# A first layer of 20 block products a pair instead of 22, chained over PSUM banks

## The chip, the cores and the metric

The kernel runs on one core of a Trainium2 chip (trn2). TensorE is called PE here, VectorE DVE, ScalarE ACT, GpSimd POOL and SyncE SP. The metric is the time of one execution in microseconds (us), as the median of several runs on the device.

## The reference

Two stages in float32. The first is a linear attention with the delta rule, for 4 batches of 8 heads, 768 steps and 48 features a head. Its output is laid out as 3072 tokens of 384 features. The second is a feed-forward network with a gate, of width 2048:

```python
for t in range(S):
    kt, vt, bt = (k_n[:, :, t], v[:, :, t], beta[:, :, t, None])
    y[:, :, t] = np.einsum('bhd,bhde->bhe', q[:, :, t], state)
    v_old = np.einsum('bhde,bhd->bhe', state, kt)
    state = state + bt[:, :, :, None] * np.einsum('bhd,bhe->bhde', kt, vt - v_old)
...
h = x @ w_in            # 3072 x 384 by 384 x 2048
g = h * np.cos(h)
return (g @ w_out)      # 3072 x 2048 by 2048 x 384
```

## The kernel before

**Tiling.** The 768 steps are cut into 24 units of 32 steps; a unit of all 4 batches is 128 tokens. Two units make a pair: 12 pairs of 256 tokens.

**The attention, by units.** `turn` and `gram` on PE make the products of keys and queries. The grams go through DRAM (`gram_put`, `gram_get`) into a tile `gb`, and POOL inverts a triangular matrix for two units at once: `invert`, whose lines L765 and L772 run one after the other for each of 32 columns in narrowing shapes, in a tile `z` that ACT first sets to the identity (L744). The result goes through DRAM again (`put`, L786, then `get`, L805) into `zt`, and PE runs `solve`, `update` and `within`, and `features`, which turns the result into `x_ffn`, the input of the network: three blocks of 128 features for each of the pair's two units. Inversion m serves the units 2m and 2m+1. SP issues most transfers; 16 stand on ACT's queue.

**The network, by pairs.** The first layer's weights `w_in` are three rows (k = 0 to 2) of sixteen 128x128 tiles. They come in parts: the load is split, shifted and added together, the last of it on POOL (L547), which does the same for `w_out`. Pairs 0 and 1 run the first layer plainly (`hidden`, L965: for each of 8 groups of four tiles, twelve matmuls into one PSUM bank). Pairs 2 to 11 use a bilinear scheme: tiles are taken four at a time, as one block of 128 by 512, so that a product is four 128x128 matmuls into one bank. In the trace one float32 matmul shows as two records. A plain pair would take 24 such products. The scheme takes 11 for each half `s` of the width, 22 in all. For it, sums of blocks of x are made for each pair (`x_sum`, L1046, four DVE operations on 128x128) and sums of weight blocks once (`in_sums`, L1061, eight DVE operations on 128x512). `layer` (L1084) runs the products of step i, `layer_out` copies a bank into the gate tile on ACT (L1100) or adds the gate tile and a bank on DVE (L1103), so that partial sums are used more than once.

**Gating and the second layer.** Each 128x512 block of h then goes through `turns` on ACT (L1005), `rest` on DVE (L1012), `cos` on ACT (L1021) and `gate` on DVE (L1024). The second layer of pair 0 is plain (`output`, L1110); the other pairs use seven products instead of eight (`product`, L1167, each in two halves of four matmuls of 128x192; sums of gate blocks on DVE, L1183; `collect`, L1217).

**PSUM.** Eight banks: two for `kq`, two for `two`, three for `h` (the first layer's), one for `o`.

**Order.** Every piece of work is a task with an engine, a cost and what it depends on. `Order.run` plays them through at build time as a list scheduler with due times, small corrections for each kind of task, and a set of tasks on ACT's queue. The order in which it starts them is the order in which they are emitted, and each engine keeps its own. So PE's order mixes first-layer products of a pair, second-layer halves of the pair before, and attention steps of later units.

Of the kernel before, what the change touches and what calls it, by code (L numbers as in the profile page):

```python
# [11 lines left out]
FP = mybir.dt.float32  # L12
# [5 lines left out]
C = 32  # L18
# [29 lines left out]
class Order:  # L48

    WINDOW = 1261.351
    LAG = {"PE": 0.2, "DVE": 0.15, "ACT": 0.15, "POOL": 0.2, "SP": 2.0, "IN": 0.0}


    RING, ISSUE, LANES = 128, 0.49, 8
    DESCRIPTORS = {
        "weights": 8, "gram_put": 64, "gram_get": 4, "put": 128, "blocks": 32, "store": 8,
        "store_left": 8, "store_right": 8,
    }

    STEADY, LATE = 130.0, {'SP': 0.66, 'POOL': 1.21, 'ACT': 0.3, 'DVE': 0.15}
    SLOW, WARM = 1.7, 4.0
    STICK = 2.528  # L70
    CHANGE = 0.17

    EARLY, NUDGE = 6, {('hidden', True): 61.2, ('out', False): 7.4, ('layer', False): 5.9, ('within', False): -4.5, ('hidden', 0, 8): 32.3, ('right', True): -39.1, ('inv', 0, 3): 5.0, ('solve_out', True): -66.4, ('turn', False): 28.3, ('rest', False): 22.3, ('rest', True): -14.8, ('state', False): -8.9, ('layer', True): 9.7, ('solve', True): 4.8, ('left', True): -6.1, ('left', False): 11.8, ('weigh', False): 11.0, ('cos', True): -11.4, ('inv', True): 4.0, ('update', False): -3.7, ('gate', False): 5.6}


    ON_ACT = {('weights', 9): 1, ('gram_put', 0): 1, ('weights', 14): 1, ('weights', 3): 1, ('gram_get', 1): 1, ('k', 7): 1, ('k', 4): 1, ('q', 3): 1, ('weights', 10): 1, ('gram_get', 2): 1, ('weights', 15): 1, ('weights', 5): 1, ('weights', 17): 1, ('weights', 6): 1, ('put', 0): 1, ('gram_get', 0): 1}
    HOLD = {('v', 5): 82.16, ('k', 8): 77.57, ('add', 9): 86.94, ('norms', 1, 1): 28.35, ('rest', 0, 2): 87.09, ('k', 6): 50.8, ('gate', 0, 4): 90.29, ('split', 11): 68.31, ('shift', 4): 40.04, ('eye', 1): 46.45, ('weights', 14): 75.83, ('features', 1): 93.82, ('split', 8): 56.33, ('split', 10): 65.61, ('get', 2): 96.99, ('half_out', 0): 53.13, ('split', 13): 77.98, ('shift', 5): 40.52, ('gram', 0): 16.72, ('norms', 2, 0): 49.12, ('add', 10): 91.37, ('add', 8): 66.01, ('right', 2): 94.14, ('q', 5): 52.19, ('add', 3): 36.15, ('square', 1, 0): 17.78, ('gram_queries', 2): 46.41, ('shift', 1): 23.89, ('shift', 16): 96.85, ('hidden', 0, 0): 70.69, ('gram_queries', 1): 23.15, ('split', 17): 99.7, ('add', 12): 77.47, ('get', 3): 101.36, ('weigh', 1): 61.19, ('v', 2): 42.92, ('eye', 2): 99.51, ('weights', 2): 18.93, ('gram_put', 2): 29.69, ('hidden', 0, 4): 80.59, ('turn_out', 1): 13.43, ('shift', 9): 60.15, ('weights', 1): 13.99, ('gram_keys', 3): 39.3, ('scale', 0, 0): 13.88, ('square', 3, 0): 65.52, ('turn', 0): 9.1, ('weigh', 0): 44.66, ('scale', 0, 1): 14.96}
    PAIRED = (
        "square", "sum", "norms", "scale", "weigh", "gram_get", "eye", "inv", "inv_out", "put",
        "x_sum", "layer", "layer_out", "turns", "rest", "cos", "gate", "out", "left", "collect",  # L80
        "store", "out_out",
    )
    SMALL = ("solve_half", "between", "gram", "state", "solve", "update", "within")


    BLOCK, PHASE, AHEAD, FETCH = 256, 63, 38, 3.5
    COUNT = {
        "turn": 16, "gram": 128, "state": 256, "solve": 128, "solve_half": 128, "between": 128, "update": 64, "within": 128,
        "features": 6, "hidden": 48, "out": 16,
    }  # L90

    def __init__(self, bufs, free):
        self.bufs, self.free = bufs, free
        self.tasks, self.users, self.tiles = {}, {}, {}
        self.written, self.rest, self.there = 0, 0.0, {}

    def add(
        self, key, engine, cost, emit, deps=(), makes=(), uses=(), moves=0.0, due=1e9
    ):

        assert key not in self.tasks, key
        if key in self.ON_ACT:
            assert moves
            engine = "ACT"
        self.tasks[key] = [engine, cost, due, emit, set(deps), makes, uses, moves]
        for t in uses:
            self.users[t] = self.users.get(t, 0) + 1
        for tag, t in makes:
            self.tiles[t] = tag

    def count(self, key):
        if key == ("state", 0):
            return 0
        if key[0] == "layer":
            return 32 if key[3] in (1, 6, 7) else 16
        return self.COUNT[key[0]]

    def descriptors(self, key):
        n = self.DESCRIPTORS.get(key[0], 16)
        if key[0] in ("k", "gram_put") and key[1] >= 8:  # L120
            n //= 2
        return n

    def stall(self, key, now, commit):

        n = count = self.count(key)

        n = int(n * 1.034 if self.written < 1000 else n * 1.0054 + self.rest)
        cost, stall, there = self.tasks[key][1], 0.0, {}
        for i in range(self.written + 1, self.written + n + 1):  # L130
            t = now + cost * (i - self.written) / n + stall
            if (i + self.PHASE + self.AHEAD) % self.BLOCK == 0:
                there[(i + self.PHASE + self.AHEAD) // self.BLOCK + 1] = (
                    t + self.FETCH + (1.5 if t < self.STEADY else 0.0)
                )
            if (i + self.PHASE) % self.BLOCK == 0:
                block = (i + self.PHASE) // self.BLOCK
                stall += max(0.0, there.get(block, self.there.get(block, 0.0)) - t)
        if commit:
            if self.written >= 1000:  # L140
                self.rest += count * 1.0054 - n
            self.written += n
            self.there.update(there)
        return stall

    def run(self, wrote):
        waiting, heirs, ready = {}, {}, {e: [] for e in self.LAG}
        for key, task in self.tasks.items():
            waiting[key] = len(task[4])
            for d in task[4]:  # L150
                heirs.setdefault(d, []).append(key)

        left = {key: len(heirs.get(key, ())) for key in self.tasks}
        ends = [key for key, n in left.items() if n == 0]
        for key in ends:
            engine, cost, due, *_, moves = self.tasks[key]
            for d in self.tasks[key][4]:
                t = self.tasks[d]
                t[2] = min(t[2], due - t[1] - self.LAG[t[0]] - t[7])
                left[d] -= 1  # L160
                if left[d] == 0:
                    ends.append(d)
        for key, task in self.tasks.items():
            n = key[1] if len(key) > 1 and isinstance(key[1], int) else 0
            if key[0] in self.PAIRED:
                n *= 2
            task[2] += self.NUDGE.get((key[0], n < self.EARLY), 0.0) + self.NUDGE.get(key, 0.0)
        for count, (key, task) in enumerate(self.tasks.items()):
            if not task[4]:
                heapq.heappush(ready[task[0]], (task[2], count, key))  # L170
        live = {tag: 0 for tag in self.bufs}
        left = dict(self.users)
        free = {e: self.free.get(e, 0.0) for e in self.LAG}
        flights, accepted, hot = [(7.0, 7.5, 8, "SP")] * self.LANES, {}, 1e9
        running, small = {}, False
        events = [(t, 0, None, False) for t in sorted({0.0, *free.values(), *self.HOLD.values()})]
        heapq.heapify(events)
        count, now = len(self.tasks), 0.0
        log = []
        while events:  # L180
            now, _, key, done = heapq.heappop(events)
            if key is not None:
                if done:
                    del running[key]
                    for t in self.tasks[key][6]:
                        left[t] -= 1
                        if left[t] == 0:
                            live[self.tiles[t]] -= 1
                engine, moves = self.tasks[key][0], self.tasks[key][7]
                for h in heirs.get(key, ()):  # L190

                    near = self.tasks[h][0] == engine and not moves
# [1458 lines left out]
```

## Time and profile before

Three runs: 670.58, 672.70 and 676.12 us.

| What | before |
|---|---|
| median of the runs | 672.70 us |
| profiled execution, first to last instruction (span) | 668.2 us; the page has no other time of this execution |
| TensorE clock granted, mean | 0.998 |
| PE busy, MATMUL records | 615.3 us (92%), 12120 |
| DVE busy, instructions | 470.1 us (70%), 892 |
| ACT busy, instructions | 246.2 us (37%), 416 |
| POOL busy, instructions | 348.5 us (52%), 734 |
| DMA moved | 51.8 MB, mean 78 GB/s |

How to read it. A group's line gives the source line, engine, operation, output and inputs, shape, count, then the busy time and the mean of one in ns, then the idle time of that engine just before, with what ended it. Records of PE overlap, so the mean of one is longer than the time from one to the next. The chain is the work that ended last, followed back from the end. In the slices a digit is tenths of busy time, 40 slices of 16.7 us each. A line of the waits gives what waited and for what, then total us, times, and the longest. In the timeline, the first number is the start, the second the duration.

### The profile page before, as it was taken

Reading aid. Unit: us, or ns where it says so; the run is one execution under the profiler, and the core shown is the slowest. Engines: PE = TensorE matmul, PEld = TensorE weight load, DVE = VectorE, ACT = ScalarE, POOL = GpSimd, SP = SyncE. Lnnn points to the kernel's source line nnn. Section 1 sums busy time; section 2 is a strip of 40 time slices with the busy share of each in tenths; the row PEclk is TensorE's granted clock in tenths of the full one; section 3 lists DMA queues with packets and bytes.
Section 4 is the critical chain, followed back from the end, with each engine's and each line's share of the span. In section 5 each row is a group of like instructions: output and inputs, shape, how many; then the busy total and the mean of one; then the engine's idle time right before and its main releaser. Section 6 shows DMA issues by size and latency. Waiting matters only on the chain.

```text
span 668.2 us, 27726 instructions
## 1 busy us (share of the span) xinstructions
PE 615.3 (92%) x12120; PEld 576.3 (86%) x12120; DVE 470.1 (70%) x892; ACT 246.2 (37%) x416; POOL 348.5 (52%) x734
## 2 busy tenths in 40 slices
PE   3316999999999999999999999999999999999997
PEld 3315878887989998999999999989999999989996
DVE  6695679788775875977866867767667656656661
ACT  3433545651243342433434334333324324323420
POOL 4458788978728628458438477158077067000000
PEclk9999999999999999999999999999999999999999
DMA  8866764574455244344434343342311311100000
GB/s 174 205 162 147 180 150 118 135 126 68 73 97 83 51 80 76 53 87 75 64 70 72 67 79 60 63 79 46 71 29 44 50 27 34 25 3 26 1 25 24
DMA packets 215645, 51.80 MB, mean 78 GB/s; under 512 B 207076, under 2 KB 210420, under 8 KB 215524
## 3 DMA queue, kind: packets, MB, share of 16 engines
q1 hardware_dynamic: 204516, 43.39, 34.4%
q10 hardware_dynamic: 10752, 6.20, 3.5%
q8 instruction: 95, 1.56, 1.0%
q0 software_dynamic: 256, 0.44, 0.3%
q14 instruction: 26, 0.21, 0.1%
HBM read 39.24 MB, written 10.75 MB: 75 GB/s over the span
## 4 chain that ended last, share of the span: by engine, by line
PE 82%; POOL 5%; DMA 5%; DVE 4%; issue 2%; ACT 1%; SPq 1%; ACTq 0%; DVEq 0%; POOLq 0%
PE p_h L1084 31%; PE p_out L1167 29%; PE p_kq L822 4%; PE p_h L965 3%; PE p_out L1110 3%; PE p_s L908 2%; PE p_u L885 2%; PE p_kq L925 2%; PE p_g L655 2%; POOL part L765 2%; POOL z L772 2%; PE p_o L1167 2%; PE p_z L944 1%; DMA g_dr<-g 1%; DMA qp<-in_q_dram 1%
## 5 line engine op out<-in xcount | busy, mean ns | idle before, releaser
L765 POOL TENSOR_TENSOR part<-z,gb 128x126 f32<-128x126 f32 (+22 forms) x341 | 135.8, 398 | 134.5 <-DMA gb<-g_dr 77.9
L772 POOL TENSOR_TENSOR z<-z,part 128x126 f32<-128x126 f32 (+22 forms) x341 | 138.5, 406 | 26.7
L1084 PE MATMUL p_h<-x_ffn,w_in 128*128 128x128 f32 x1120 | 145.5, 277 | 1.0 <-issue 1.0
L1084 PEld LDWEIGHTS p_h<-x_ffn,w_in 128*128 128x128 f32 x1120 | 135.5, 192 | 3.7 <-issue 2.1
L1167 PE MATMUL p_out<-w_out,g_ffn 128*128 128x192 f32 x672 | 122.9, 327 | 0.3 <-issue 0.3
L1005 ACT ACTIVATE turns<-p_h,quarter_turn 128x512 int32<-128x512 f32 x96 | 66.0, 687 | 150.3 <-DVE p_h L1103 106.9
L1167 PEld LDWEIGHTS p_out<-w_out,g_ffn 128*128 128x128 f32 x672 | 107.6, 190 | 1.0 <-issue 0.6
L1167 PE MATMUL p_out<-w_sum,g_ffn 128*128 128x192 f32 x496 | 91.3, 329 | 0.0
L1021 ACT ACTIVATE turns<-turns,halfpi 128x512 f32<-128x512 f32 x96 | 69.1, 721 | 42.3 <-DVE turns L1012 40.9
L1012 DVE SCALAR_TENSOR_TENSOR turns<-p_h,turns 128x512 f32<-128x512 f32 x96 | 65.6, 683 | 26.9 <-ACT turns L1005 26.8
L1167 PEld LDWEIGHTS p_out<-w_sum,g_ffn 128*128 128x128 f32 x496 | 79.4, 190 | 1.0
L1183 DVE TENSOR_TENSOR g_ffn<-g_ffn 128x512 f32<-128x512 f32 x88 | 61.9, 704 | 14.8 <-PE p_out L1167 13.9
L1100 ACT COPY g_ffn<-p_h 128x512 f32<-128x512 f32 x60 | 35.2, 586 | 96.4 <-PE p_h L1084 96.1
L1103 DVE TENSOR_TENSOR p_h<-g_ffn,p_h 128x512 f32<-128x512 f32 x60 | 41.7, 695 | 38.6 <-PE p_h L1084 37.8
L1024 DVE TENSOR_TENSOR g_ffn<-turns,p_h 128x512 f32<-128x512 f32 x96 | 64.9, 678 | 5.5 <-POOL w_out L547 3.3
L576 POOL TENSOR_TENSOR knrm<-ksum,halves 128x16 f32<-128x16 f32 (+1 forms) x14 | 37.3, 2665 | 39.8 <-DVE ksum L564 39.8
L965 PE MATMUL p_h<-x_ffn,w_in 128*128 128x128 f32 x384 | 47.7, 283 | 1.5 <-POOL w_in L547 1.3
L965 PEld LDWEIGHTS p_h<-x_ffn,w_in 128*128 128x128 f32 x384 | 45.3, 196 | 2.7 <-POOL w_in L547 1.7
L1217 DVE SCALAR_TENSOR_TENSOR o<-p_out,o 128x192 f32<-128x192 f32 x74 | 25.3, 354 | 29.5 <-PE p_out L1167 29.0
L1084 PE MATMUL p_h<-x_sum,in_sum 128*128 128x128 f32 x320 | 43.1, 278 | 0.7 <-issue 0.7
L1084 PEld LDWEIGHTS p_h<-x_sum,in_sum 128*128 128x128 f32 x320 | 40.2, 191 | 1.4 <-issue 0.8
L624 PE MATMUL p_t<-consts,kp 128*128 128x128 f32 x32 | 7.4, 373 | 31.8 <-DMA halves_z<-z_dr 19.4
(110 smaller groups left out, 780.4 us busy)
## 6 DMA issues: line engine op xcount, KB each, us to landing
pairs<-in_moe_w_out_dram SPq DMA_DIRECT2D x13, 384.0 KB
vp<-in_v_dram SPq DMA_DIRECT2D x96, 48.0 KB
gb<-g_dr SPq DMA_DIRECT2D x18, 256.0 KB
out_dram<-o SPq DMA_DIRECT2D x23, 192.0 KB
pairs<-in_moe_w_in_dram SPq DMA_DIRECT2D x7, 512.0 KB
kp<-in_k_dram SPq DMA_DIRECT2D x128, 24.0 KB
z_dr<-z SPq DMA_DIRECT2D x11, 256.0 KB
zt<-z_dr SPq DMA_DIRECT2D x88, 32.0 KB
```

The costliest lines, as they stand in the source:

```text
L576: nc.gpsimd.tensor_tensor(out=scales[m][2][:, part], in0=sums[m, part.start][:, 0:n], in1=halves[:, 0:n], op=ALU.pow,)
L765: eng.tensor_tensor(out=part, in0=z[:, 0:rows, j, None].to_broadcast(shape), in1=a[:, j, None, j + 1 :].to_broadcast(shape), op=ALU.mult,)
L772: eng.tensor_tensor(out=behind, in0=behind, in1=part, op=ALU.subtract)
L965: nc.tensor.matmul(p_h[:, i], w_in[:, t, (4 * k + i) * 128 : (4 * k + i + 1) * 128], xts[p][:, t, unit * 128 : (unit + 1) * 128], start=(t ...
L1005: nc.scalar.activation(turns[p, f], hidden_of(p, f), AF.Identity, bias=quarter_turn, scale=TURN)
L1012: nc.vector.scalar_tensor_tensor(out=r, in0=hidden_of(p, f), scalar=TURN, in1=t, op0=ALU.mult, op1=ALU.subtract,)
L1021: nc.scalar.activation(r, r, AF.Sin, bias=halfpi, scale=2.0 * math.pi)
L1024: nc.vector.tensor_tensor(out=place(p, f), in0=step_of(rests.pop((p, f)), f), in1=step_of(hidden_of(p, f), f), op=ALU.mult,)
L1084: nc.tensor.matmul(p_h[:, e], in_sum[:, odd_tile, 4 * s + e] if a == "s" else w_in[:, a, f * 128 : (f + 1) * 128], x_sums[p][:, unit] if b ...
L1103: nc.vector.tensor_tensor(out=block(p, s, 0, 1) if i == 3 else p_h, in0=block(p, s, *one), in1=p_h, op=ALU.add,)
L1167: nc.tensor.matmul(p_o, left(p, part, a)[:, e % 4], right(e, b), start=(e == 0), stop=(e == FT // 2 - 1), skip_group_check=True,)
L1183: nc.vector.tensor_tensor(out=left(p, s, to), in0=left(p, s, one), in1=left(p, s, two), op=op)
```

## The change

- A pair's first layer takes 20 products instead of two halves of 11. `FACTORS` names for each product its weight block and its block of x; `STEPS` gives the sequence of products, copies and adds. The products run into banks "a" to "g" and "o", and a bank that has been copied out, or filled by a copy from another bank, is added to by later products.
- Nine copies a pair on ACT (six before), some from bank to bank, some with a factor of -1; ten adds or subtractions on DVE (eight before), most of them into the gate tile. One block of eight is gated in its bank, the other seven in the gate tile.
- `x_sum` becomes eleven operations of 128x128 for each pair, on POOL, into eleven buffers (`XS`).
- `in_sums` becomes 22 operations of 128x512 on DVE, once; fourteen of them write into `w_in` itself, after the last plain first layer.
- `gb` and `z` have one buffer instead of two (`GBS`, `ZS`).
- `Order` no longer plays the tasks through: `LINE` lists their numbers in the order in which they are emitted, and `OTHER` the tasks that go to another queue or engine. `OTHER` holds the same 16 transfers as `ON_ACT` before.
- In the last pair, second-layer products that use an `h` bank come after the last first-layer product.
- In the listed order, PE runs four plain `hidden` between inversion 1 and `solve` of unit 2 (six, and one `output`, before), and inside inversion 1 POOL adds two slices of weights (four before).

```diff
-    GBS, ZS = 2, 2
+    GBS, ZS = 1, 1
+    XS = 11
...
-        t = x_sums[p] = ffn_pool.tile([128, 3, 128], FP, name="x_sum", bufs=1)
...
-            nc.vector.tensor_tensor(out=to, in0=one, in1=two, op=ALU.subtract)
...
+    X_SUMS = {
+        "d": ("b0", "a0"), "n": ("b0", "b1"), "m": ("d", "b1"), "e": ("m", "a1"),
+        "k": ("e", "a2"), "g": ("b2", "k"), "i": ("n", "k"), "l": ("b2", "d"),
+        "f": ("a2", "l"), "h": ("f", "a1"), "b0": ("b2", "b0"),
+    }
...
+        either(("x_sum", p, x), nc.gpsimd, nc.vector).tensor_tensor(
+            out=to, in0=one, in1=two, op=op
+        )
...
-    STEPS = {
-        0: [(0, 0, 0, 0)],
-        1: [(1, 0, 1, 0), (2, 0, 2, 0)],
-        2: [("s", 0, "t", 0)],
-        3: [("s", 1, "t", 1)],
-        4: [(0, 1, 0, 1)],
-        5: [(2, 1, 2, 1)],
-        6: [("s", 2, 1, 1), (2, 0, 2, 1)],
-        7: [(1, 1, "t", 2), (2, 1, 2, 0)],
+    FACTORS = {
+        0: ((1, 2), "f"), 1: ((1, 1), "g"), 2: (S7, "a0"), 3: (S3, "h"), 4: ((0, 1), "i"),
+        5: ((3, 1), "e"), 6: (S4, "b0"), 7: ((1, 0), "d"), 8: ((0, 2), "a2"), 9: (S2, "k"),
+        10: ((2, 2), "i"), 11: (S5, "l"), 12: ((3, 2), "g"), 13: (S6, "m"), 14: ((2, 0), "b2"),
+        15: (S0, "a0"), 16: ((3, 0), "b1"), 17: ((2, 1), "a1"), 18: (S1, "d"), 19: ((0, 0), "n"),
     }
...
+    STEPS = [
+        (18, "c"), ("c", (3, 1), -1.0), (1, "c"), ("c", (1, 1), -1.0),
+        (15, "b"), ("b", "a", 1.0), (4, "b"), ("b", "o", 1.0), (10, "a"), ("a", (2, 0), 1.0),
+        (8, "o"), (9, "b"), ("b", (3, 0), 1.0), (3, "a"), ((2, 1), (1, 1), ALU.subtract, "a"),
+        (12, "b"), ((3, 1), "b", ALU.subtract, (3, 1)), (6, "a"),
+        ((1, 1), (1, 1), ALU.subtract, "a"), (11, "d"), ("d", (1, 0), 1.0), (0, "a"),
...
+    def layer(p, x, to, new):
+        w, b = FACTORS[x]
+        p_h = part_of(p, to, new)
+        for e in range(4):
+            nc.tensor.matmul(
+                p_h[:, e],
+                in_block(*w)[:, e],
+                x_of(p, b),
+                start=new and e == 0,
+                stop=True,
+                skip_group_check=True,
+            )
+
+    def layer_copy(p, one, to, by, new):
+        to = part_of(p, to, new)
+        if by == 1.0:
+            nc.scalar.copy(to, part_of(p, one))
         else:
+            nc.scalar.activation(to, part_of(p, one), AF.Copy, scale=by)
+
+    def layer_add(p, to, one, op, two):
+        nc.vector.tensor_tensor(
+            out=part_of(p, to), in0=part_of(p, one), in1=part_of(p, two), op=op
+        )
...
-    log = order.run(wrote)
+    order.run(wrote)
```

A step of `STEPS` that begins with a number is a product and its bank; three entries are a copy (from, to, factor); four are an add or subtraction (to, one, operation, two). A tuple such as (3, 1) is a block of h in the gate tile: group of four tiles, unit.

## The prediction

> **What bounds the kernel now.** I read the page's first two parts first, to see which engine is full and when.
>
> ```profile
> PE 615.3 (92%) x12120; PEld 576.3 (86%) x12120; DVE 470.1 (70%) x892; ACT 246.2 (37%) x416; POOL 348.5 (52%) x734
> PE   3316999999999999999999999999999999999997
> POOL 4458788978728628458438477158077067000000
> PEclk9999999999999999999999999999999999999999
> PE 82%; POOL 5%; DMA 5%; DVE 4%; issue 2%; ACT 1%; SPq 1%; ACTq 0%; DVEq 0%; POOLq 0%
> ```
>
> PE is full from the fifth slice (about 67 us) to the end, at a granted clock that never falls under nine tenths. The last line, the chain that ended last, is 82% PE. POOL is half free, with gaps. So in the ten bilinear pairs a matmul less is time less, unless the new order makes PE wait. Next the groups, for what a product and its helpers cost, and the waits, to see whether anything holds PE.
>
> ```profile
> L1084 PE MATMUL p_h<-x_ffn,w_in 128*128 128x128 f32 x1120 | 145.5, 277 | 1.0 <-issue 1.0
> L1084 PE MATMUL p_h<-x_sum,in_sum 128*128 128x128 f32 x320 | 43.1, 278 | 0.7 <-issue 0.7
> L1100 ACT COPY g_ffn<-p_h 128x512 f32<-128x512 f32 x60 | 35.2, 586 | 96.4 <-PE p_h L1084 96.1
> L1103 DVE TENSOR_TENSOR p_h<-g_ffn,p_h 128x512 f32<-128x512 f32 x60 | 41.7, 695 | 38.6 <-PE p_h L1084 37.8
> PE p_t L624 <- DMA halves_z<-z_dr: 19.4, 1, 19.4
> PE p_h L1084 <- issue: 2.4, 3, 1.0
> POOL part L765 <- DMA gb<-g_dr: 77.9, 6, 21.4
> ```
>
> The copies of L1100 and the adds of L1103 wait for PE (96.1 and 37.8 us); PE waits for neither. PE's only large wait is 19.4 us once, at the start. POOL's inversions wait for their input, not PE for them. The mean of 277 ns is not the price of a matmul, since records overlap. The chain of waits prices whole pieces:
>
> ```profile
> 186.48 1.30 PE p_out L1167 x8
> 187.79 1.78 PE p_h L1084 x16
> ```
>
> Eight records are one first-layer product; here two of them take 1.78 us, 0.111 a record. Half a second-layer product takes 1.30.
>
> **Removed.** Ten pairs lose 2 of 22 products each: 10 x 2 x 8 = 160 records x 0.111 = **-17.8 us**. By busy time per record instead (L1084's groups together 232.3 us over 1760 records, 0.132) it would be -21.1. I take the first, which is elapsed time.
>
> **More work between products.** Before, a half needs three copies and four adds; after, a whole pair needs 9 copies on ACT (6 before) and 10 adds on DVE (8). ACT gains 30 x 0.586 = 17.6 us and stays near 40%. DVE's account: 40 small subtractions leave with x_sum (15.1 us), 20 adds come (20 x 0.695 = 13.9) and 14 more in_sums (14 x 0.69 = 9.7): +8.5, to about 479. Seven of a pair's eight gatings now read SBUF, not PSUM: 140 operations at L1183's 704 ns instead of 678 to 683, some 3 us more on DVE. Neither becomes the bound as a sum. The risk is single waits. A chained product may start only when the copy that frees or fills its bank is done; in the written order I counted the matmuls that stand between. Before, the tightest place has 1.78 us of cover for a copy; after, it is one half product (1.30), and 33 places have under 2 us: 23 on an ACT copy, 10 on a DVE add. What the cover must hide is in the timeline:
>
> ```profile
> 630.33 1.73 PE L1084 MATMUL p_h<-x_sum,in_sum 128*128 128x128 f32 x14
> 631.20 0.59 ACT L1100 COPY g_ffn<-p_h 128x512 f32<-128x512 f32 x1
> 631.89 0.82 PE L1167 MATMUL p_out<-w_sum,g_ffn 128*128 128x192 f32 x4
> ```
>
> The first of these products ends near 631.0, the copy starts 0.2 later and takes 0.59, and I allow as much again for the way back: 1.0, or 1.1 by a DVE add. That fits into 1.30 if the engine is free. ACT is busy 40% of the time, with half a turn (0.35) to go on average: 23 x 0.4 x 0.1 = 0.9. DVE is busy 70%: 10 x 0.7 x 0.1 = 0.7. I take **+1.5**. Bounds: 0, and 33 x 0.5 = +16.5 if each finds a whole 0.7 us operation ahead of it. With no cover at all 90 copies would cost about 0.9 each, 81 us; the cover is the other layer's matmuls standing between in the new order.
>
> **in_sums.** The 14 new ones stand on DVE while the first bilinear pairs begin, and the windows show least room there:
>
> ```profile
> 100.00:120.00 20.00, 19.45 (x520) 16.90 (x520) 17.66 (x32) 12.22 (x23) 16.46 (x34) 1.00 0.49 130
> 140.00:160.00 20.00, 19.42 (x159) 13.15 (x161) 17.73 (x31) 6.32 (x12) 14.42 (x23) 1.00 0.72 116
> 300.00:320.00 20.00, 20.00 (x334) 19.32 (x320) 15.19 (x28) 7.70 (x13) 16.94 (x40) 1.00 0.42 72
> ```
>
> Columns are length, then PE, PEld, DVE, ACT, POOL busy. DVE has 2 to 4 us free in each 20. Behind each in_sum queue the gates of the plain pairs, and behind these the second layer on PE. With 60 us to spread over the cost is 0; with none it is 9.7. I take **+0.5**, near the free end.
>
> **x_sum moved to POOL.** Four DVE operations a pair become eleven on POOL. POOL has no row of this exact operation; the inversions' subtraction of the same size is nearest, and DVE's old row beside it:
>
> ```profile
> L1046 DVE TENSOR_TENSOR x_sum<-x_ffn 128x128 f32<-128x128 f32 x20 | 7.3, 363 | 2.5 <-ACT x_ffn L952 1.9
> L772 POOL TENSOR_TENSOR z<-z,part 128x128 f32<-128x128 f32 x11 | 5.0, 459 | 0.9
> ```
>
> 110 x 0.459 is 50.5 us, at the 0.53 from start to start 58: POOL goes from 348 to about 400 of 655, by itself no bound. But POOL runs in order, and the x_sums of pairs 2 to 10 stand behind most of an inversion, of pairs 4 and 5 behind a whole one (inversions 5 and 6). This closes a loop: the gram on PE, its way through DRAM, the inversion, an x_sum, and the product that reads it.
>
> ```profile
> 330.21 0.86 PE L655 MATMUL p_g<-kq_t 48*32 48x64 f32 x64
> 344.10 0.24 POOL L765 TENSOR_TENSOR part<-z,gb 128x31 f32<-128x31 f32 x1 [18.45 <-ACT turns L1021]
> 373.08 0.23 POOL L772 TENSOR_TENSOR z<-z,part 128x16 f32<-128x16 f32 x1
> ```
>
> From gram to first step 13.9 us (12.4 after the next gram), 29.2 of inversion, 0.5 of x_sum: 42.1 to 44.3 with the slowest inversion, 29.9. Against it stands PE's own work between that gram and the product that needs the sum: 18 first-layer products (16.1), 12 half products (15.6), 3 state steps (3.9), 2 grams (1.4), solves, updates and features (5.2) and switches, about 43. So each of the two pairs is between 0.9 early and 1.3 late; the others have 1 to 3 us more. I take **+0.5**; bounds 0 and 2.2 x 10 = 22, if all ten pairs paid the whole spread.
>
> [...]
>
> [...]
>
> **One buffer for gb and z instead of two.** The next inversion's input can load only when the last inversion is done. In the steady pairs this is so already:
>
> ```profile
> 282.73 0.54 SPq L786 DMA_DIRECT2D z_dr<-z  x1
> 285.98 0.49 SPq L728 DMA_DIRECT2D gb<-g_dr  x1
> ```
>
> The put of one inversion is issued first, the next gb load behind it. So **0**; bound 4.8, the one place where the trace shows the load earlier than that, by that much.
>
> **The start.** In inversion 1 POOL loses its additions of the late w_in and w_out slices: 6.7 us of additions and waits stood inside it, 2.5 stay, so it ends some 4.1 earlier. But PE, which used to run six plain products and one output ahead of solve(2), now runs four, 5.5 + 2.9 = 8.4 us less cover.
>
> ```profile
> 92.73 2.11 SPq L805 DMA_DIRECT2D zt<-z_dr  x4
> 94.91 5.52 PE L965 MATMUL p_h<-x_ffn,w_in 128*128 128x128 f32 x48
> 100.36 0.88 PE L885 MATMUL p_u<-rhs,zt 32*32 32x48 f32 x64
> ```
>
> The solve needs these four loads. Issued by 94.84, and at 4.75 to 4.87 a transfer as the chain's first DMA pieces show, they land near 99.6, so PE had almost no slack. A wait of 8.4 - 4.1 - 0.7 = 3.6 is to be expected there, but work taken from in front of a wait is done later in a place where PE would else idle, and PE is busy 16.4 and 18.0 of the 20 us windows around. I take **+1.5**, between -4.1 and +8.4.
>
> **Sum.** -17.8 + 1.5 + 0.5 + 0.5 + 0 + 1.5 = -13.8. The profiled span is 668.2, so 654.4. The page gives no other time of that execution; the median of the runs, 672.7, is 4.5 above the span, and with it the forecast is **658.9 us**.
>
> **Rivals.**
> 1. *The start loses its cover.* The put and the loads stand on SP's queue behind weights, so the inversion's 4.1 are not passed on and all 8.4 show: 658.9 + 6.9 = 665.8. For it: the 0.7 us of slack. Against: SP's issues of kp held the put from 85.7 to 88.35 before, and need not again.
> 2. *The narrow waits take the gain back.* Each of 33 finds an operation ahead of it: 16.5 instead of 1.5, 673.9. For it: DVE at 70%, ACT's order fixed with turns that wait for DVE. Against: PE waited for neither engine at covers of 1.78, and 1.30 still exceeds 1.0.
> 3. *The POOL loop sets the period: slower.* With one z and one gb the next load waits for the put to have read z, and x_sums queue behind the later inversion. If every pair pays the 4.8 us above, less 2 us of slack, it is 10 x 2.8 = 28 in place of 0.5: 686.4. From 1.4 us a pair nothing of the gain is left, from 2.05 it is slower by over 1%. For it: cover and chain are equal within 1 us in two pairs. Against: in eight pairs the sums stand ahead of the last columns, and POOL waits 77.9 us for input now.
> 4. *Less is removed than said.* The calls in the product line fall from 880 to 800 and no switch between small and large matmuls is added (166, then 164), so I leave this out.
>
> **How the numbers follow.** Forecast 0.72, rival 1 0.11, rival 2 0.09, rival 3 0.08. One per cent is 6.7 us, and the three runs (670.58 to 676.12) can hardly tell less. Faster by that means under 666.0: the forecast and half of rival 1, 0.78. Within it: the rest of rival 1 and rival 2, 0.14. Slower, over 679.4: 0.08. The range goes from 651 (-21.1 with all additions free is 651.6) to 668 (rival 1 with 2 us more in narrow waits), and leaves out rivals 2 and 3, 0.17.
>
> **What would show it.** MATMUL records 11960 and PE busy about 595 to 600; the product line's records 1600 at the same 0.11 each along the chain; in PE's waits, under 3 us in sum on the layer's copies and adds and under 2 on x_sum; POOL near 400 with the sums at 0.45 to 0.5; a wait at solve(2) of 0 to 4 us; in_sums on DVE without a later PE idle. I am wrong if PE idles between pairs on POOL or on gb, if waits on ACT and DVE pass 10 us, or if the late start shows whole at the end.

## The result and the profile after

The changed kernel takes 665.99 us (median of nine runs, 663.04 to 668.82), the kernel before 671.73 beside it (nine runs). The ratio is 0.9915, 95% interval [0.9893, 0.9937]: 5.7 us faster, 0.85%. The forecast was 658.9, 13.8 below the 672.70 of the first three runs; so the direction and the range held, and less than half of the forecast gain is there. The products did go: 160 records, worth an estimated 17.8 us at the 0.111 us a record of before. The question is what took 12 us back.

The page of the changed kernel's profile (span 666.3 us, of a run of 668.13), busy times, two rows of the 40 slices, the granted clock, and the chain that ended last:

```profile
PE 604.3 (91%) x11960; PEld 565.6 (85%) x11960; DVE 487.5 (73%) x886; ACT 261.4 (39%) x446; POOL 448.5 (67%) x844
PE   4317689999989999989999999999999999999997
POOL 4378766888898878858858858968658679403000
PEclk9999698999989999989999999999999999999999
PE 45%; POOL 32%; DMA 9%; issue 6%; DVE 4%; ACT 1%; SPq 1%; ACTq 0%; POOLq 0%; DVEq 0%
```

Three things are new. POOL has 100 us more, where 50 to 58 were expected. The chain runs over POOL for 32% of the span (5% before). And the clock, which was at nine tenths or more in all slices, falls to 6 in the fifth, and to 8 in three more.

The groups that answer to those of before: the layer's products (of three forms, one shown), a copy on ACT, the adds on DVE, then what was not expected: POOL's two inversion lines, its sums, and the gating on DVE.

```profile
L1054 PE MATMUL p_h<-x_sum,w_in 128*128 128x128 f32 x640 | 85.5, 282 | 4.2 <-POOL x_sum L969 3.4
L1066 ACT COPY p_h<-p_h 128x512 f32<-128x512 f32 x40 | 22.9, 573 | 32.5 <-PE p_h L1054 31.6 <-DVE g_ffn L1071 0.7
L1071 DVE TENSOR_TENSOR g_ffn<-g_ffn,p_h 128x512 f32<-128x512 f32 x80 | 54.4, 682 | 23.8 <-PE p_h L1054 19.6 <-ACT g_ffn L1068 2.2 <-ACT g_ffn L1066 1.1
L676 POOL TENSOR_TENSOR part<-z,gb 128x126 f32<-128x126 f32 (+22 forms) x341 | 148.8, 436 | 66.6 <-DMA gb<-g_dr 27.0
L683 POOL TENSOR_TENSOR z<-z,part 128x126 f32<-128x126 f32 (+22 forms) x341 | 157.5, 462 | 26.7
L969 POOL TENSOR_TENSOR x_sum<-x_sum,x_ffn 128x128 f32<-128x128 f32 x40 | 23.9, 599 | 2.1
L924 DVE SCALAR_TENSOR_TENSOR turns<-g_ffn,turns 128x512 f32<-128x512 f32 x70 | 53.1, 767 | 5.9 <-ACT turns L917 5.9
L936 DVE TENSOR_TENSOR g_ffn<-turns,g_ffn 128x512 f32<-128x512 f32 x70 | 52.9, 764 | 6.9 <-ACT turns L933 6.8
L936 DVE TENSOR_TENSOR g_ffn<-turns,p_h 128x512 f32<-128x512 f32 x26 | 17.6, 679 | 4.7 <-POOL w_out L458 2.7 <-ACT turns L933 2.0
```

Copies and adds still wait for PE, as before. But the same inversions, step for step, take 306.3 us in sum (148.8 + 157.5) where they took 274.3. A gate that reads its block from SBUF takes 764 ns, one that reads a PSUM bank 679. A sum on POOL takes 0.6 us.

PE's waits in the network and at the start:

```profile
PE p_h L1054 <- POOL x_sum L969: 5.7, 4, 2.3
PE p_v L763 <- ACT u_half L773: 3.4, 2, 2.8
PE p_u L796 <- DVE u_half L781: 3.3, 2, 2.6
PE p_u L796 <- DMA zt<-z_dr: 1.2, 1, 1.2
```

None is for a copy or an add of the layer. Where they stand, in the timeline of PE (start, length, then what it waited for):

```profile
66.93 4.63 PE L876 MATMUL p_h<-x_ffn,w_in 128*128 128x128 f32 x24
74.32 1.50 PE L763 MATMUL p_v<-u_half,halves_z 32*32 32x48 f32 x64 [2.76 <-ACT u_half L773]
78.41 1.50 PE L796 MATMUL p_u<-u_half,halves_z 32*32 32x48 f32 x64 [2.59 <-DVE u_half L781]
185.67 1.29 PE L1054 MATMUL p_h<-x_sum,in_sum 128*128 128x128 f32 x8 [2.04 <-POOL x_sum L969]
195.34 2.84 PE L1054 MATMUL p_h<-x_sum,w_in 128*128 128x128 f32 x24
285.71 4.48 PE L1054 MATMUL p_h<-x_sum,w_in 128*128 128x128 f32 x24 [2.29 <-POOL x_sum L969]
```

In the kernel before, a plain product stood between the halves of each first solve, and PE had no such gap:

```profile
51.76 1.50 PE L852 MATMUL p_v<-u_half,halves_z 32*32 32x48 f32 x64 [0.62 <-ACT u_half L862]
69.20 4.26 PE L965 MATMUL p_h<-x_ffn,w_in 128*128 128x128 f32 x24
73.39 0.88 PE L852 MATMUL p_v<-u_half,halves_z 32*32 32x48 f32 x64
74.20 2.94 PE L965 MATMUL p_h<-x_ffn,w_in 128*128 128x128 f32 x24
77.08 0.88 PE L885 MATMUL p_u<-u_half,halves_z 32*32 32x48 f32 x64
```

The profile's clock is 1.00 for all of these rows, but ahead of its first change it can't be taken at its word: the same 64 records take 1.50 us at 51.76 and 0.88 at 73.39, and the first `hidden` has six or seven records in each us up to 72 us and eleven in the next. So the kernel before, too, runs at half speed at 51.76 and again from 69 to 72 us, and its clock is 1.00 in every us from 72 to 665. The changed kernel has 0.50 again from 74 to 84 us, behind its two gaps, and both solves take 1.50. All six other profiles with the changed kernel's order on PE at the start have a stretch at 0.50 there, of 7 to 10 us between 74 and 87; in inv_short the second solve, at 77.38 behind a wait of 3.16, takes 1.50. The long first `hidden` is no loss of the change: 4.26 us before, 4.63 after.

The two long waits in the bilinear pairs cost more than their length. The three products at 195.34 take 2.84 us, the three at 285.71, behind a wait of 2.29, take 4.48. The windows after the wait at 185.67 show why; the figure behind POOL's busy time is the clock:

```profile
182.00:184.00 2.00, 1.63 (x172) 1.49 (x158) 1.62 (x5) 0.00 (x0) 1.76 (x4) 1.00 0.38 64
186.00:188.00 2.00, 2.00 (x12) 2.00 (x11) 0.00 (x0) 0.94 (x2) 1.69 (x6) 0.64 0.45 78
188.00:190.00 2.00, 2.00 (x46) 1.56 (x49) 0.00 (x0) 0.39 (x1) 1.61 (x6) 0.51 0.54 130
190.00:192.00 2.00, 2.00 (x54) 1.91 (x42) 1.28 (x2) 0.00 (x0) 1.61 (x6) 1.00 0.15 27
```

So there are two losses: one before 110 us, and one over POOL in the bilinear pairs. Twelve runs take them apart.

### The profile page after: what moved, and what is told of

It reads as the page before. It is cut to its first block, busy times and chain, and to the rows that moved or that the text cites. A ratio compares the mean times of both kernels' runs of the same rounds, so it can differ in the third digit from the quotient of the medians.

```text
span 666.3 us, 27542 instructions
## 1 busy us (share of the span) xinstructions
PE 604.3 (91%) x11960; PEld 565.6 (85%) x11960; DVE 487.5 (73%) x886; ACT 261.4 (39%) x446; POOL 448.5 (67%) x844
## 4 chain that ended last, share of the span: by engine, by line
PE 45%; POOL 32%; DMA 9%; issue 6%; DVE 4%; ACT 1%; SPq 1%; ACTq 0%; POOLq 0%; DVEq 0%
PE p_out L1134 17%; PE p_h L1054 16%; POOL z L683 13%; POOL part L676 13%; POOL x_sum L969 4%; PE p_h L876 3%; DMA gb<-g_dr 3%; DMA qp<-in_q_dram 2%; PE p_kq L733 2%; PE p_u L796 2%; PE p_o L1134 2%; PE p_s L819 1%; PE p_kq L836 1%; DMA zt<-z_dr 1%; PE p_out L1077 1%
## 5 line engine op out<-in xcount | busy, mean ns | idle before, releaser
L676 POOL TENSOR_TENSOR part<-z,gb 128x126 f32<-128x126 f32 (+22 forms) x341 | 148.8, 436 | 66.6 <-DMA gb<-g_dr 27.0
L683 POOL TENSOR_TENSOR z<-z,part 128x126 f32<-128x126 f32 (+22 forms) x341 | 157.5, 462 | 26.7
L1054 PE MATMUL p_h<-x_sum,w_in 128*128 128x128 f32 x640 | 85.5, 282 | 4.2 <-POOL x_sum L969 3.4
L1054 PEld LDWEIGHTS p_h<-x_sum,w_in 128*128 128x128 f32 x640 | 79.2, 195 | 6.0 <-POOL x_sum L969 3.8
L917 ACT ACTIVATE turns<-g_ffn,quarter_turn 128x512 int32<-128x512 f32 x70 | 50.2, 721 | 67.3 <-DVE g_ffn L1071 52.1
L1071 DVE TENSOR_TENSOR g_ffn<-g_ffn,p_h 128x512 f32<-128x512 f32 x80 | 54.4, 682 | 23.8 <-PE p_h L1054 19.6
L936 DVE TENSOR_TENSOR g_ffn<-turns,g_ffn 128x512 f32<-128x512 f32 x70 | 52.9, 764 | 6.9 <-ACT turns L933 6.8
L924 DVE SCALAR_TENSOR_TENSOR turns<-g_ffn,turns 128x512 f32<-128x512 f32 x70 | 53.1, 767 | 5.9 <-ACT turns L917 5.9
L876 PE MATMUL p_h<-x_ffn,w_in 128*128 128x128 f32 x384 | 48.9, 289 | 0.0
L876 PEld LDWEIGHTS p_h<-x_ffn,w_in 128*128 128x128 f32 x384 | 47.2, 204 | 1.0
L1054 PE MATMUL p_h<-x_ffn,w_in 128*128 128x128 f32 x320 | 43.7, 280 | 0.0
L1054 PEld LDWEIGHTS p_h<-x_ffn,w_in 128*128 128x128 f32 x320 | 39.2, 191 | 1.1
```

Of the source, the lines that this page charges most:

```text
L676: eng.tensor_tensor(out=part, in0=z[:, 0:rows, j, None].to_broadcast(shape), in1=a[:, j, None, j + 1 :].to_broadcast(shape), op=ALU.mult,)
L683: eng.tensor_tensor(out=behind, in0=behind, in1=part, op=ALU.subtract)
L876: nc.tensor.matmul(p_h[:, i], w_in[:, t, (4 * k + i) * 128 : (4 * k + i + 1) * 128], xts[p][:, t, unit * 128 : (unit + 1) * 128], start=(i ...
L917: nc.scalar.activation(turns[p, f], hidden_of(p, f), AF.Identity, bias=quarter_turn, scale=TURN)
L924: nc.vector.scalar_tensor_tensor(out=r, in0=hidden_of(p, f), scalar=TURN, in1=t, op0=ALU.mult, op1=ALU.subtract,)
L936: nc.vector.tensor_tensor(out=place(p, f), in0=step_of(rests.pop((p, f)), f), in1=step_of(hidden_of(p, f), f), op=ALU.mult,)
```

## The experiments

All times are ratios to the kernel before, run beside them.

| Kernel | median us | ratio, 95% interval |
|---|---|---|
| changed kernel | 665.99 | 0.9915 [0.9893, 0.9937] |
| start_hidden | 662.90 | 0.9887 [0.9862, 0.9912] |
| start_put | 667.30 | 0.9948 [0.9927, 0.9969] |
| start_get | 669.01 | 0.9959 [0.9936, 0.9982] |
| xsum_dve | 658.05 | 0.9810 [0.9784, 0.9836] |
| xsum_dve_248 | 665.01 | 0.9898 [0.9866, 0.9929] |
| inv_short (4 columns) | 657.95 | 0.9804 [0.9765, 0.9842] |
| inv_short3 (3 columns) | 656.83 | 0.9796 [0.9759, 0.9833] |
| dve_hidden | 656.07 | 0.9751 [0.9718, 0.9785] |
| dve_hidden_again | 655.26 | 0.9759 [0.9739, 0.9780] |
| dve_start | 658.76 | 0.9806 [0.9774, 0.9838] |
| copy_twice | 659.67 | 0.9824 [0.9800, 0.9848] |
| before_sbuf (the kernel before, edited) | 674.89 | 1.0059 [1.0036, 1.0081] |

### All sums on DVE

```diff
     OTHER = {
+        ('x_sum', 2, 'b0'), ('x_sum', 2, 'd'), ...   # all 110 tasks
```

> The changed kernel with all 110 x_sums on DVE instead of POOL, in the same places of the written order. Theory C (x_sums queue on POOL behind the inversions: PE waited 5.7 us for them in 4 places and then ran at half clock): the waits of the layer's products on x_sum end, POOL falls from 448 to about 390 us, DVE rises from 487 to about 528, and the time falls by 4 to 8 us to 658 to 662. Theory D (DVE is short already, in the stretches around the first bilinear pairs above all): the same 40 us of work reappear as waits of PE on gates and adds of DVE, and the time is the same or up to 8 us longer.

658.05 us: theory C. PE waits for no sum any more, and the chain is PE again:

```profile
PE 599.6 (91%) x11960; PEld 561.7 (86%) x11960; DVE 506.6 (77%) x996; ACT 261.8 (40%) x446; POOL 385.1 (59%) x734
PE 76%; POOL 8%; DMA 6%; DVE 5%; issue 2%; ACT 1%; SPq 1%; ACTq 0%; DVEq 0%; POOLq 0%
L971 DVE TENSOR_TENSOR x_sum<-x_sum,x_ffn 128x128 f32<-128x128 f32 x40 | 13.4, 336 | 0.5
L685 POOL TENSOR_TENSOR z<-z,part 128x126 f32<-128x126 f32 (+22 forms) x341 | 160.8, 471 | 26.7
```

So the sums on POOL cost about 7 us (0.9915 against 0.9810). In the rows shown one takes 0.34 us on DVE, 0.60 on POOL. The inversions are as long as in the changed kernel (160.8 us in the second line); DVE, at 77%, does not become the bound, against theory D.

### Only the pairs that were seen waiting

> The changed kernel with the x_sums of pairs 2, 4 and 8 alone on DVE (33 of 110), those whose products PE was seen waiting for; the others stay on POOL. With all on DVE the time was 658.05 us, 7 less than the changed kernel. Theory C1 (the loss lies in the few places where a product waits for a sum behind an inversion): at least 4 of the 7 us come back, 659 to 662, and the waits on x_sum fall from 5.7 to under 2 us. Theory C2 (every x_sum on POOL pushes the next inversions and so the whole chain; a wait removed in one pair comes back in the next): the waits move to other pairs, and the time stays within 2.5 us of 666.

665.01 us, 1 us less by the ratio, with some 2.5 us to either side: theory C2 in time, and the 4 us of theory C1 lie just outside. The waits on x_sum fell from 5.7 to 2.2 us in sum, nearly as C1 had it, but both that are left stand in pair 5, where there had been none:

```profile
322.70 1.16 PE L1056 MATMUL p_h<-x_sum,in_sum 128*128 128x128 f32 x8 [1.02 <-POOL x_sum L971]
327.21 1.16 PE L1056 MATMUL p_h<-x_sum,w_in 128*128 128x128 f32 x8 [1.16 <-POOL x_sum L971]
```

The places where PE was seen waiting were not the whole of the loss. That POOL sets a pace, which PE meets now here and now there, fits this, but is argued. The profiled execution is also the fastest of the six (661.84 us).

### What makes the inversions longer

```diff
     def hidden_of(p, f):
-        return p_hs[(p, f[0], HOME[f[1:]]) if isinstance(f, tuple) else (p, f)]
+        return block(p, *f) if isinstance(f, tuple) else p_hs[p, f]
```

> The kernel before, with one thing changed: the gating of the ten bilinear pairs reads its block from the gate tile in SBUF instead of the PSUM bank (turns, rest and gate of all eight blocks a pair, so 80 rests and 80 gates have two SBUF inputs); the values gated are then partial sums, not h. Theory E (two-input SBUF operations on DVE and POOL's inversions slow each other): the inversions' rows, 274 us in sum before and 306 in the changed kernel, come to 300 to 315, the mean of rest and gate from 683 and 678 to 740 to 780 ns; since POOL had slack before, the time rises by less than 4 us. Theory F (the changed kernel's inversions are slower because of the x_sums and transfers around them): the rows stay at 270 to 280 us and rest and gate under 710 ns.

Theory E. In the kernel before, with nothing changed but where the gating reads, the rows of DVE and POOL become those of the changed kernel:

```profile
L1012 DVE SCALAR_TENSOR_TENSOR turns<-g_ffn,turns 128x512 f32<-128x512 f32 x80 | 58.9, 743 | 0.0
L1024 DVE TENSOR_TENSOR g_ffn<-turns,g_ffn 128x512 f32<-128x512 f32 x80 | 58.0, 726 | 1.3 <-ACT turns L1021 1.3
L765 POOL TENSOR_TENSOR part<-z,gb 128x126 f32<-128x126 f32 (+22 forms) x341 | 150.1, 440 | 116.8 <-DMA gb<-g_dr 91.6
L772 POOL TENSOR_TENSOR z<-z,part 128x126 f32<-128x126 f32 (+22 forms) x341 | 156.2, 458 | 26.7
```

150.1 + 156.2 = 306.3 us, the sum of the changed kernel. That it meets to the tenth is chance: here 80 rests and 80 gates read SBUF alone, there 70 and 70, and POOL has the sums as well. The time rises by 0.6%, 4 us, at the edge of what was expected; where these 4 us lie was not taken apart.

Both sides grow by what was changed: the 80 gates that read SBUF take 726 ns, and the 16 that still read a PSUM bank 678, as before; POOL's steps go from 402 to 449 ns on average (274.3 and 306.3 us over 682). By what mechanism is not shown.

### Is it this length that made the sums cost?

```diff
         for j in columns:
+            if m >= HALVED and j in (12, 13, 14, 15):
+                continue
             rows, last = j // SPLIT + 1, C
```

> The changed kernel, with four of the 31 columns (12 to 15) left out of each inversion from the second on, so that each is about 4 us shorter: about what the two-input operations of DVE add to it (29 us before, 33 in the kernel with x_sums on DVE). The inversion is then incomplete, and the values with it. The x_sums stay on POOL in their places. Theory G (the length of the loop over POOL decides: with inversions as long as in the kernel before, x_sums on POOL would have cost next to nothing, as forecast): waits of PE on x_sum fall from 5.7 to under 2 us and 4 to 7 us come back, 659 to 662. Theory H (the x_sums' own length and their places in the row decide: six of them, at 0.62 us and more, stand ahead of the second product): at least 3.5 us of waits stay, and the time stays at 664 or more.

> As the kernel with four columns left out of each inversion, with three (12 to 14) instead, so that the inversions come to the length that they had in the kernel before. Four columns made inversion 5 last 26.5 us, where it was 28.2 before and 31.4 in the changed kernel, so that run went some 2 us beyond what the two-input operations had added. Three should give 27.7 to 28. If the length of before is enough for x_sums on POOL to cost next to nothing: waits on x_sum under 2 us, 658 to 660.5. If the loop needed the last 1 to 2 us as well: 2 to 4 us of waits, 661 to 664.

Both say yes. Inversion 5, from its first step to the end of its last, holds no sum inside in any of these kernels: 28.2 us before (249.07 to 277.25), 31.4 after, 26.5 with four columns left out, and with three 27.7; inversion 6 lasts 29.6, 32.9, 27.0 and 29.4. So three columns give back the length of before. The sums stay on POOL at about 0.6 us, in their places, and the time is 656.83 us, no longer than with all sums on DVE. PE's waits on x_sum are 1.1 us with either. Both times lie some 1 us below the ranges expected. With inversions as long as before, the sums on POOL cost next to nothing, as the forecast said; with 3 us more in each inversion they cost 7 in the whole.

### The start: plain products one slot earlier

```diff
 # order on PE, pair 0's plain products written (0, f)
-solve_half(1) hidden(0,0) between(1) solve(1) update(1) within(1) hidden(0,2) ... hidden(0,4) hidden(0,6) solve(2)
+solve_half(1) hidden(0,0) hidden(0,2) between(1) hidden(0,4) solve(1) update(1) within(1) ... hidden(0,6) hidden(0,8) solve(2)
```

> The changed kernel with one thing moved in the written order: the plain first-layer pieces hidden(0,2) to hidden(0,14) stand one slot earlier on PE, so that one runs ahead of between(1) and one ahead of solve(1), as in the kernel before; the gating of hidden(0,4) moves up with them. Theory A (the start lost its cover: PE waited 2.76 and 2.59 us there, its granted clock fell to 0.50 from 66 to 69 and from 75 to 84 us, and a hidden then took 4.6 us instead of 2.9): both waits become less than 0.5, the clock stays at 1.0 from 70 us on, and the time falls from 666.0 by 4 to 8 us, to 658 to 662. Theory B (the start is set by transfers and inversion 1, whatever PE does meanwhile): solve of unit 2 stays at 99 to 100 us and the idle time only moves behind the hidden pieces; the time stays within 1.5 us of 666.0.

662.90 us; 0.9887 against 0.9915 is 2 us, less than the 4 to 8 expected, and the intervals overlap. On top of xsum_dve the same edit gives 0.9751 and 0.9759 against 0.9810, 3.4 to 4 us. The gaps close:

```profile
68.55 7.76 PE L877 MATMUL p_h<-x_ffn,w_in 128*128 128x128 f32 x48
76.27 0.88 PE L764 MATMUL p_v<-u_half,halves_z 32*32 32x48 f32 x64
77.08 2.94 PE L877 MATMUL p_h<-x_ffn,w_in 128*128 128x128 f32 x24
80.15 0.88 PE L797 MATMUL p_u<-u_half,halves_z 32*32 32x48 f32 x64
```

The two solves take 0.88 us each instead of 1.50, and none waits more than 0.7. Part of it goes again: a gap of 2.2 us comes at 87.8 us, ahead of `features`, and the clock from 90 to 100 us is 0.66 on average. And `solve` of unit 2 does not come earlier, as theory B had it: it starts at 100.42, at 99.57 in the changed kernel. What is gained is that five `hidden` are done by then instead of four, one of 2.9 us for 0.85 us of delay, which is about the 2 us measured.

### The start: the put, and the get

> The changed kernel with one thing moved in the written order: the eight loads of k for unit 9 stand on SP's queue behind the put of inversion 1 instead of ahead of it. In the changed kernel inversion 1 ended near 81 us, its put was issued only at 88.50, behind sixteen loads. Theory A (the put waits on the queue): put at 82 to 83 us, solve of unit 2 at 93 to 95 instead of 99.6, the wait on zt gone; the time falls by 2 to 5 us if PE's loss at the start lies in that wait, and by less than 1.5 if it lies ahead of it, in the waits at 74 to 81 us. Theory B (the put is late for another reason): put and solve stay where they are, and so does the time.

> The changed kernel with the eight loads of k for unit 9 behind both the put of inversion 1 and the get of unit 2 on SP's queue. With the loads moved behind the put alone, the put was issued at 81.88 instead of 88.50, but the get only at 92.0, behind the same loads, and solve of unit 2 stayed at 99.5. Theory A (the queue holds the result of inversion 1): get at 86 to 88 us, solve of unit 2 at 92 to 95, the wait for zt gone. In time: 1 to 3 us less than the changed kernel if the start is bound by this result, no difference (within 1.5 us) if PE's lack of plain products and its half clock from 63 to 84 us bind, since those are not touched.

Neither gives anything; by the ratio (0.9948 and 0.9959 against 0.9915) both are 2 to 3 us slower, start_put with intervals that overlap, and why was not taken apart. With the put alone moved, it was issued at 81.88, but the get stayed at 92.0. In the second, SP's queue shows the next thing that was in the way:

```profile
82.16 0.39 SPq L698 DMA_DIRECT2D z_dr<-z  x1
83.80 0.35 SPq L436 DMA_DIRECT2D pairs<-in_moe_w_out_dram  x1
91.34 0.38 SPq L619 DMA_DIRECT2D g_dr<-g  x1
91.81 2.03 SPq L717 DMA_DIRECT2D zt<-z_dr  x4
```

The put of gram 5 stands ahead of the get, and its gram comes from PE near 91. So the result of inversion 1 was never fetched early in these two kernels, and whether the solve would then have started earlier stays open. The part of the start's loss that a run gave back is the one that start_hidden found, in PE's order.

### Both edits, and two more steps

> Both edits that helped alone: all x_sums on DVE (658.05 us by itself) and the plain products of pair 0 one slot earlier (662.9 by itself, some 2 to 3 less than the changed kernel). If the two losses are separate, as theories A and C together say, the gains add: 654 to 657 us, PE's waits at 74 and 78 us under 1 us and none on x_sum. If the start's gain is hidden by a later wait on DVE, which now carries the x_sums too, it stays at 657 to 659.

> The same kernel with both edits as before, for the comparison with the doubled copies on the same chip, and to see whether the 656.07 us stand: 654 to 658 us.

656.07 and 655.26 us: the gains add. At 0.9751 to 0.9759 this is 16 to 17 us faster than the kernel before and 10 faster than the changed one, and the 17.8 us of the removed products are there but for 1 to 2.

> As the kernel with both edits, and besides the k loads of unit 9 behind the put of inversion 1 and the get of unit 2, and hidden(0,6) ahead of features(1), in the gap in which PE waited 2.2 us and fell to half clock from 90 to 99 us. If the start still holds 5 to 6 us of the expected gain (the lead over the kernel before fell from 17 us at 80 us to 12 at 100), 2 to 4 of them come back: 651 to 655. If w_in's last slices, added on POOL only after inversion 1 (84 to 87 us), bind, the gap stays and the time is that of the kernel with both edits within 1.5 us.

658.76, slower than without the last two steps. Here the get was early (86.77), but hidden(0,6) and its successor, moved ahead, waited 6.9 us in three places for a bank that DVE's gates had still to free, and solve of unit 2 ran at 102.5. So the products moved ahead of the gates that free their banks held PE up, and all that stands behind them on it, for these 6.9 us.

> The kernel with both edits (x_sums on DVE, plain products of pair 0 one slot earlier; 656.07 us), with each of the 90 copies of a bank on ACT done twice over. ACT gains 90 x 0.59 = 53 us. In the changed kernel no product of the layer waits for a copy or an add, which says that the cover holds; this asks by how much. If the 1.0 us from the end of a product over its copy to the next product is about all that the cover of 1.30 to 2 us has, the doubled copy (1.6) shows in the 23 narrow places with 0.2 to 0.5 us and more where ACT is busy: 5 to 12 us longer. If the cover is used up already and hidden by buffers elsewhere, 25 us or more. If it is far wider in time than the counted matmuls say, under 3 us.

659.67 against 655.26: 4.4 us for 53 us more of ACT, less than the 5 to 12 expected.

```profile
PE p_h L1056 <- ACT g_ffn L1069: 0.9, 2, 0.5
PE p_h L1056 <- ACT p_h L1069: 0.6, 1, 0.6
```

Only three products waited for a copy, 1.5 us in all. The page has a granted clock of five tenths in the second to fourth slice. That is no slower start: a solve in the fourth slice takes 1.50 us with and without the doubled copies (at 53.63, and at 52.51 in dve_hidden_again, where the clock row says 1.00). What makes up the rest of the 4.4 us was not taken apart.

## Why the prediction was right or wrong

**Removed products, -17.8: right within 1 to 2 us.** With the two losses mended, 16 to 17 us are measured, with the other terms of the sum in them.

**Narrow waits, +1.5: smaller.** In the list of PE's waits none is for a copy or an add of the layer. Rival 2 is out.

**in_sums, +0.5: nothing seen.** PE has no wait above 0.6 us between 100 and 173 us.

**x_sum on POOL, +0.5: this step failed; it measured 7.** The loop was named, with its terms, and two of them were mis-sized. The first is the inversion, taken at 29.2 us from the rows of before: inversions 5 and 6 last 31.4 and 32.9 us in the changed kernel, though no sum stands inside. The cause was in the prediction, two paragraphs earlier and at the wrong price: seven gatings of eight read SBUF, "some 3 us more on DVE". On DVE it was 12 for rests and gates (70 x 84 and 70 x 86 ns), and POOL was not looked at, where it was 32. The second is the sum, one of 0.5 us. A sum takes 0.6 us on POOL on average, and the second product of a pair (1, with block "g") hangs on five of them, one after the other (d, m, e, k, g). In pair 4, "g" is even listed last of eleven; here are the first and the last:

```profile
278.92 0.46 POOL L969 TENSOR_TENSOR x_sum<-x_ffn 128x128 f32<-128x128 f32 x1
285.20 0.45 POOL L969 TENSOR_TENSOR x_sum<-x_ffn,x_sum 128x128 f32<-128x128 f32 x1
```

The first starts as inversion 5 ends, the last ends 6.7 us later, and the product that waited 2.29 us for it starts at 285.71. inv_short3 shows that this long row of sums alone would not have mattered: it has the same sums in the same order, and with inversions as long as before PE waits 1.1 us in all. Whether the longer inversions would have mattered with "g" listed fifth is not shown; no run changed the order of the sums. Rival 3 had the loop, but with the single buffers as its price, and at 28 us.

**One buffer for gb and z, 0: not tested by itself.** POOL waits 27.0 us for gb, less than the 77.9 of before, but it also has less time to wait. Inversions 6 and 7 wait last for ACT, which sets the one z to the identity only just before (10.1 us of POOL's waits). Their first steps come 4.9 and 5.0 us after the load of gb is issued, where it was 6.6 and 4.4 before, so little can lie there. No run has two buffers again; the kernel with both edits has one, and what it lacks of the 17.8 us, 1 to 2, bounds the cost there.

**The start, +1.5: too small.** Mending PE's order gives 2 to 4 us, so the loss is at least that. Rival 1 had the mechanism half right: the put was issued at 88.50, behind sixteen loads of k, as late as before (88.35), though the inversion ended 4 us earlier, and `solve` of unit 2 came at 99.57, hardly earlier than the 100.36 of before, with four `hidden` done instead of six and an `output`. But most of PE's idle time lay ahead of that, between the halves of the first solves, where before a plain product stood in each; the wait at `solve` itself was 1.16 us. And a cost was left out altogether: behind these gaps PE ran at half clock, from 74 to 84 us, where it had full clock before.

**The base.** Runs of both kernels lie 1.8 us over their spans (for the kernel before, 672.37 us with a span of 670.6), so 2.7 of the 4.5 us were only that its profiled execution was shorter than the median.

Of the chances: the result lies in "within 1%", which had 0.14.

## What to carry to other kernels

When a change moves an operand from PSUM to SBUF, price it for the other engine that reads SBUF beside it too, not only for the one that executes it: here 140 operations on DVE grew by 12 us and POOL's inversions by 32. A duration taken from the profile of before did not hold when what ran beside it changed: inversion 5 went from 28.2 to 31.4 us, with the same steps. And a loop whose two sides are within a microsecond of each other should get the width of its range from the least certain duration in it, times the number of rounds.

## What the hardware showed that was not expected

Gaps of PE were followed by half clock: 2.04 us at 183.6, then 0.64 and 0.51 in 186 to 190; 2.29 us at 283.4, then 0.50 in 286 to 288; in start_hidden 2.19 us at 87.8, then 0.51 and 0.50 in 90 to 96. So was the gap of 1.16 us at 98.4 in the changed kernel, behind which `solve` of unit 2 begins with twelve records in 0.8 us: the clock is 0.50 in 102 to 104. A gap of 1.15 us at 478.3 was not, with 1.00 behind it. What decides was not tried.

The ratio of POOL to DVE for the same sums was 1.8 (599 ns on POOL in the changed kernel, 336 on DVE in xsum_dve, the mean of 40 of the 110), with both engines at work. The prediction's rows of before, 459 and 363 ns, had made it 1.26.
